# Decoding the first batch's weights through a PSUM bank, with attention in one bank

## The chip, the cores and the metric

One core of one Trainium2 chip. The metric is the device time of one execution in microseconds; a few runs are made and their median counts. Five engines work side by side, each through its own list of instructions in a fixed order: TensorE (matmuls), VectorE, ScalarE, GpSimd, and SyncE, which issues the DMAs. Where one needs what another makes, it waits for that engine's count of finished instructions (a semaphore). PSUM has eight banks of 128 partitions x 512 words of 32 bits; TensorE writes its results there, VectorE and ScalarE can read and write them.

## What is computed

Windowed attention (4 batches, 8 heads, 576 positions, 64 per head; four heads see a window of 32, four a dilated one of 128 by steps of 4), then a gated feed-forward block, then a second one with a PReLU:

```
attn = softmax(mask(q @ k.T / 8));  x = attn @ v            # reshaped to 2304 x 512
y    = (sigmoid(x @ w_gate) * (x @ w_val)) @ w_out           # 512 -> 1536 -> 512
h    = y @ w_in;  g = max(h, 0) + alpha * min(h, 0)          # 512 -> 2048
out  = g @ w_out2                                            # 2048 -> 512
```

The weights come as raw words, two of 32 bits for each number (the 64-bit form of it). The kernel turns them into 32-bit floats itself.

## The kernel before

**Decoding.** `decode` (L175) takes one or more blocks of 128 x 512 numbers, as pairs of a destination `d` in SBUF and the words `w`, whose low and high halves lie in turn. Three VectorE steps make a number: L179 shifts the high word left by 3 and masks it into `d`; L183 adds the two top bits of the high word to `d`; L187 adds the three top bits of the low word, shifted down. Each step is done for all blocks of the call before the next begins. The first batch decodes 36 such blocks: `dec` for the 12 column groups of the gate and value weights (two blocks each; the first group as two calls), `odec` for `w_out` (three blocks for each of four groups; the second as two calls and one). So there are 18 calls. Later batches decode `w_in` and `w_out2` with the same function.

**What follows on a decoded block.** ScalarE squares and sums it (`wb`, L194), TensorE adds that over the partitions with a matmul against ones (`wsum`, L148), VectorE makes a power of two from the sum (`wpow`, L156 and L160, then GpSimd L164), and ScalarE and GpSimd, or ScalarE and VectorE, split the scaled weights into two halves of 16 bits (`spl`, L168, L172, L204, L205). `g` and `v` are TensorE's matmuls of gate and value (L590, in two halves of 12 matmuls), `sig` and `mul` ScalarE's sigmoid and VectorE's product (L603, L608), `half` the split of the product, `o` the output matmuls (L632).

**Attention.** A head group `hb` is one of two kinds of one batch; 0 and 1 belong to the first batch, 2 and 3 to the second, and these are done while the first batch goes through its feed-forward block. `qkm hb c` puts a third of the scores into a bank (L309, L316, L323), `qks hb c` takes their maximum and subtracts it on VectorE (L354, L355), `pvm hb half` multiplies by the values for two pairs of heads (L437), and `pvx hb half pair` splits the result on ScalarE and VectorE (L171, L172).

**Banks.** Banks 0 to 5 are three double buffers for the feed-forward matmuls; the small sums of L148 sit at the end of one of them. Banks 6 and 7 are attention's, in turn (`att_bank`).

**Order.** In the first batch the order of all engines' work is written out by hand in `FIRST`, a list of tasks; each engine gets its instructions in that order. From the second batch on loops set it, and the preparation of the later weights is dealt out by a budget.

Of the kernel before, what the change touches and what calls it, by code (L numbers as in the profile page):

```python
# [1563 lines left out]
warm 8 5; lqk 0 3; lqk 1 3; lv 0; qkm 0 0; lv 1; qks 0 0; qkm 0 1; qkm 0 2; exp 0 0; qks 0 1 1; rs 0 0;  # L1564
qks 0 2 1; exp 0 1; pm 0 0 0; qkm 1 0 4; tr 0 0; rs 0 1; lgv 0; qks 1 0; pm 0 1 0; exp 0 2; rs 0 2; qkm 1 1 5;
exp 1 0; lgv 1; lqk 2; warm 6 2; lv 3; pm 0 2 0; qkm 1 2 0; lal; qks 1 1; tr 0 2; exp 1 1; xb 0; tr 0 1;
qks 1 2 1; rs 1 1; pv32 0 0 6; pm 1 1 0; xb 1; rs 1 0; xsum 0 0; exp 1 2; pm 1 0 0; pv32 0 1 4; dec 0 0; xpow 0;
rs 1 2; pm 1 2 0; tr 1 1; vhi 1 1; dec 0 1; tr 1 0; lgv 2; phi 1 1; vlo 1 1; vhi 1 0; pvx 0 1 1; warm 14 3;
tr 1 2; pvx 0 1 0; pvx 0 0 1; lv 2; wb 0; vlo 1 0; wsum 0; pvx 0 0 0; phi 1 0; plo 1 1; phi 1 2; plo 1 2 0;
plo 1 0 0; wpow 0; spl 0 0; pvm 1 1 4; pvm 1 0; dec 1; pvx 1 1 1; pvx 1 0 0; lgv 3; spl 0 1 1; pvx 1 1 0;  # L1570
g 0 0 0; wb 1; wsum 1; lgv 4; lgv 6; wgs 0; wpow 1; pvx 1 0 1; qkm 2 0; qkm 2 1; dec 2; xb 2; lgv 5; spl 1 0;
spl 1 1 1; g 0 0 1; wb 2; v 0 0 0; sig 0 0; wsum 2 0; v 0 0 1; wgs 1; wpow 2; dec 3; mul 0 0; g 0 1 0; g 0 1 1;
spl 2 0; spl 2 1 1; wb 3; wsum 3; v 0 1 0; xb 3; wpow 3; v 0 1 1; spl 3 0; sig 0 1; g 0 2 0; qks 2 1; g 0 2 1;
# [104 lines left out]
```

## Time and profile before

| | |
|---|---|
| median of 3 runs | 900.86 us (900.86 to 901.72) |
| profiled execution | 900.97 us |
| its span (first to last instruction) | 899.2 us |
| TensorE busy | 850.2 us (95%) |
| VectorE busy | 681.9 us (76%) |
| ScalarE busy | 450.4 us (50%) |
| GpSimd busy | 304.6 us (34%) |

All rows below are of the one profiled execution; times count from the start of its span, and 1.8 us of the execution lie outside the span. Busy time is an average over the whole span, and the stretches differ much, so the rows are of stretches. Durations of instructions that follow each other on one engine overlap a little in the records where neither waits for the other.

### The profile page before, as it was taken

The numbers are of one execution on the slowest core, as the hardware profiler recorded it, in microseconds if no ns is written. First come the engines' busy times: TensorE is split into PE (matmuls) and PEld (weight loads), VectorE is DVE, ScalarE is ACT, GpSimd is POOL, SyncE is SP. The second block draws the span as 40 slices with busy tenths as digits, with TensorE's granted clock in tenths as the row PEclk, the third lists the DMA queues.
The fourth block names the chain that finished last, engine by engine and source line by source line (L and its number), as shares of the span: only waits on it lengthen the run. The fifth ranks groups of instructions, "written<-read, shape, count | busy, mean of one in ns | idle before, by whom it ended". The sixth has DMA issues, their size and how long they took to land.

```text
span 899.2 us, 19438 instructions
## 1 busy us (share of the span) xinstructions
PE 850.2 (95%) x8196; PEld 701.5 (78%) x8196; DVE 681.9 (76%) x1039; ACT 450.4 (50%) x739; POOL 304.6 (34%) x264
## 2 busy tenths in 40 slices
PE   7879789799999999999999989997899999999998
...
GB/s 323 266 212 151 121 141 158 58 28 141 139 51 182 144 74 195 62 1 230 266 180 219 300 279 195 347 218 184 265 236 188 240 322 188 199 274 203 142 214 83
DMA packets 85176, 166.81 MB, mean 186 GB/s; under 512 B 5345, under 2 KB 57697, under 8 KB 85089
## 3 DMA queue, kind: packets, MB, share of 16 engines
...
q14 instruction: 24, 0.19, 0.1%
...
## 4 chain that ended last, share of the span: by engine, by line
PE 57%; DVE 26%; ACT 6%; issue 4%; DMA 4%; POOL 1%; SPq 1%; ACTq 0%; DVEq 0%; POOLq 0%
PE banks L590 14%; PE banks L1207 14%; PE banks L964 13%; PE banks L632 12%; DVE plain L183 4%; DVE plain L187 3%; PE banks L437 3%; DVE plain L179 2%; DVE temp_w L1010 2%; DVE temp_y L1010 1%; DVE gf L608 1%; DVE halves L824 1%; DMA words<-w_gate 1%; DVE g_gv L1049 1%; PE banks L323 1%
## 5 line engine op out<-in xcount | busy, mean ns | idle before, releaser
L590 PE MATMUL banks<-xh,w_gv 128*128 128x288 f16 x2304 | 297.7, 291 | 1.5 <-ACT sg L603 1.5
L590 PEld LDWEIGHTS <-w_gv 128*128 128x128 f16 x2304 | 226.1, 99 | 62.6 <-issue 1.8
L964 PE MATMUL banks<-yh,w_i 128*128 128x256 f16 x1536 | 189.9, 275 | 12.1 <-ACT temp_y L1019 6.4
L964 PEld LDWEIGHTS <-w_i 128*128 128x128 f16 x1536 | 151.3, 99 | 32.5 <-issue 12.3
L632 PE MATMUL banks<-gt,w_o 128*128 128x288 f16 x1152 | 149.5, 291 | 1.0 <-POOL gt L168 0.9
L632 PEld LDWEIGHTS <-w_o 128*128 128x128 f16 x1152 | 113.5, 100 | 31.9 <-issue 1.1
L1207 PEld LDWEIGHTS <-g_gv 128*128 128x128 f16 x780 | 76.7, 98 | 9.1
L1207 PE MATMUL banks<-w,g_gv 128*128 128x256 f16 x612 | 75.5, 273 | 0.0
L164 POOL TENSOR_SCALAR sc<-sc 128x1 f32<-128x1 f32 x35 | 12.4, 354 | 180.7 <-DVE sc L160 180.6
L1059 POOL TENSOR_TENSOR yh<-temp_y 128x512 f32<-128x512 f32 x16 | 27.0, 1689 | 131.6 <-DVE temp_y L1010 126.9
L194 ACT ACTIVATE junk<-plain 128x1024 bf16<-128x1024 f32 (+1 forms) x36 | 36.4, 1010 | 60.4 <-DVE plain L198 32.1
L1010 DVE SCALAR_TENSOR_TENSOR temp_w<-neg,sc,temp_w 128x256 f32<-128x256 f32 x48 | 55.5, 1195 | 10.9 <-ACT neg L1002 10.8
L187 DVE SCALAR_TENSOR_TENSOR plain<-words,plain 128x512 uint32<-128x512 uint32 x68 | 61.9, 931 | 1.2
L183 DVE SCALAR_TENSOR_TENSOR plain<-words,plain 128x512 uint32<-128x512 uint32 x68 | 59.3, 893 | 1.2
L1207 PEld LDWEIGHTS <-g_g 128*128 128x128 f16 x564 | 55.2, 98 | 6.4
L168 POOL TENSOR_TENSOR gt<-gf,gt 128x576 f16<-128x576 f32 x24 | 36.8, 1533 | 65.2 <-ACT gt L615 65.2
L608 DVE SCALAR_TENSOR_TENSOR gf<-banks,sg 128x576 f32<-128x576 f32 x48 | 36.0, 750 | 29.3 <-PE banks L590 28.9
L603 ACT ACTIVATE sg<-banks,sc 128x576 f32<-128x576 f32 x48 | 35.2, 734 | 35.1 <-PE banks L590 24.7
L615 ACT ACTIVATE gt<-gf 128x576 f16<-128x576 f32 x48 | 32.3, 675 | 38.3 <-DVE gf L608 38.3
L1207 PE MATMUL banks<-w,g_g 128*128 128x256 f16 x396 | 48.3, 273 | 0.0
L179 DVE TENSOR_SCALAR plain<-words 128x512 uint32<-128x512 uint32 x68 | 40.2, 612 | 8.9 <-DMA plain_dram<-plain 5.5
L388 POOL TENSOR_TENSOR s<-s,rs 128x1152 f32<-128x1152 f32 (+1 forms) x9 | 17.8, 1975 | 71.7 <-DVE rs L383 64.4
...
## 6 DMA issues: line engine op xcount, KB each, us to landing
...
```

The source lines that it names most:

```text
L168: engine.tensor_tensor(out=lo, in0=src, in1=hi, op=ALU.subtract)
L179: nc.vector.tensor_scalar(out=d, in0=hi, scalar1=3, scalar2=0x3FFFFFFF, op0=ALU.logical_shift_left, op1=ALU.bitwise_and)
L183: nc.vector.scalar_tensor_tensor(out=d, in0=hi, scalar=0xC0000000, in1=d, op0=ALU.bitwise_and, op1=ALU.bitwise_or)
L187: nc.vector.scalar_tensor_tensor(out=d, in0=lo, scalar=29, in1=d, op0=ALU.logical_shift_right, op1=ALU.bitwise_or)
L194: nc.scalar.activation(junk[:, :src.shape[1]], src, AF.Square, accum_out=dst)
L590: nc.tensor.matmul(ps[:, h, :], lhsT=a, rhs=x_[:, H2 * h:H2 * h + H2], start=(kk == 0 and i == 0), stop=(kk == KD - 1 and i == 2),)
L603: nc.scalar.activation(halves(sg), ps, AF.Sigmoid, scale=sgx[b][:, m:m + 1])
L608: nc.vector.scalar_tensor_tensor(out=halves(gf), in0=ps, scalar=2.0 ** -15, in1=halves(sg), op0=ALU.mult, op1=ALU.mult)
L632: nc.tensor.matmul(ps[:, h, :], lhsT=a, rhs=x_[:, H2 * h:H2 * h + H2], start=(m == 0 and z == 0), stop=(m == M1 - 1 and z == 2),)
L964: nc.tensor.matmul(o, lhsT=h, rhs=l, start=(new and v == 0 and q == 1), stop=(q == total_), skip_group_check=True,)
L1010: nc.vector.scalar_tensor_tensor(out=temps[x_][:, c], in0=t[:, c], scalar=slope[:, u + v:u + v + 1], in1=src[:, c], op0=ALU.mult, op1=ALU.add,
L1207: nc.tensor.matmul(ps[:, H4 * t:H4 * t + H4].rearrange("p (c f) -> p c f", c=2), lhsT=a, rhs=x_, start=(first and k == 0 and t == 0 and z ...
```

## The change

In the first batch (`turn["first"]`) `decode` works on one block after the other. It cuts each block into two halves of 256 columns, and the words wait in a PSUM bank between the steps: the first step writes the bank, the second reads and writes it, the third reads it and writes the destination in SBUF. The two halves alternate step by step. The bank is number 2 for the first calls and number 6 from the task `one` on, which stands before the scores of head group 2; from there to the task `one 0`, near the end of `FIRST`, attention has bank 7 alone. Later batches decode as before.

```diff
@@ -91,7 +91,7 @@
 
 
     banks = psum.tile([P, 8, 512], F32, name="banks")
-    turn = {"m": -1, "a": -1, "h": -1, "first": True}
+    turn = {"m": -1, "a": -1, "h": -1, "first": True, "words": 2, "one": False}
 
     holds = {}
     begun = set()
@@ -120,7 +120,7 @@
 
     def att_bank(key, spare=None):
         if spare is None:
-            turn["a"] = (turn["a"] + 1) % 2
+            turn["a"] = 1 if turn["one"] else (turn["a"] + 1) % 2
             spare = 6 + turn["a"]
         hold(spare, key)
         waiting.add(key)
@@ -175,6 +175,26 @@
     def decode(*pairs):
 
         pairs = [(d.bitcast(U32), w[:, :, :, 0], w[:, :, :, 1]) for d, w in pairs]
+        if turn["first"]:
+
+            hold(turn["words"], "words")
+            t = banks[:, turn["words"], :].bitcast(U32).rearrange("p (k f) -> p k f", k=4)
+            for pair in pairs:
+                parts = [(t[:, k:k + 2],) + tuple(x_[:, k:k + 2] for x_ in pair) for k in (0, 2)]
+                for t_, d, lo, hi in parts:
+                    nc.vector.tensor_scalar(
+                        out=t_, in0=hi, scalar1=3, scalar2=0x3FFFFFFF, op0=ALU.logical_shift_left,
+                        op1=ALU.bitwise_and,
+                    )
+                for t_, d, lo, hi in parts:
+                    nc.vector.scalar_tensor_tensor(
+                        out=t_, in0=hi, scalar=0xC0000000, in1=t_, op0=ALU.bitwise_and, op1=ALU.bitwise_or
+                    )
+                for t_, d, lo, hi in parts:
+                    nc.vector.scalar_tensor_tensor(
+                        out=d, in0=lo, scalar=29, in1=t_, op0=ALU.logical_shift_right, op1=ALU.bitwise_or
+                    )
+            return
         for d, lo, hi in pairs:
             nc.vector.tensor_scalar(
                 out=d, in0=hi, scalar1=3, scalar2=0x3FFFFFFF, op0=ALU.logical_shift_left, op1=ALU.bitwise_and
@@ -420,16 +440,16 @@
         pv_mm(hb, half)
         pv_x(hb, half)
 
-    def pv_mm(hb, half, spare=None):
+    def pv_mm(hb, half, spare=None, only=None):
         b, kind = divmod(hb, 2)
         v_ = vh[hb]
         first, last = (0, NB // 2) if half == 0 else (NB // 2, NB)
         ops = [(m, max(m, first), min(m + 2, last)) for m in range(max(first - 1, 0), last)]
-        tiles = []
-        for pair in range(2):
+        tiles = xt.setdefault((hb, half), [None, None])
+        for pair in range(2) if only is None else (only,):
             k = slice(64 * pair, 64 * pair + 64)
             ps = att_bank(("pv", hb, half, pair), None if spare is None else spare + pair)[:, :H2]
-            tiles.append(ps)
+            tiles[pair] = ps
             for z, (m, n0, n1) in enumerate(ops):
                 p_ = [p_half(hb, i, WINDOW * (m + n0 + 1), WINDOW * (m + n1 + 1))[k] for i in range(2)]
                 w = [v_[k, i, m].rearrange("p h d -> p (h d)") for i in range(2)]
@@ -438,7 +458,6 @@
                         ps[:, WINDOW * (n0 - first):WINDOW * (n1 - first)], lhsT=a, rhs=x_,
                         start=(z == 0 and i == 0), stop=(z == len(ops) - 1 and i == 2), skip_group_check=True,
                     )
-        xt[hb, half] = tiles
 
     def pv32_mm(hb, half, spare):
 
@@ -1242,6 +1261,11 @@
 
     engines = (nc.gpsimd, nc.vector)
 
+    def one_bank(on=1):
+
+        turn["one"] = bool(on)
+        turn["words"] = 6
+
     def part(i):
         return whole if i is None else thirds[i]
 
@@ -1267,6 +1291,8 @@
         "vhi": v_hi,
         "vlo": v_lo,
         "pvm": pv_mm,
+        "pvo": lambda hb, half, only: pv_mm(hb, half, None, only),
+        "one": one_bank,
         "pv32": pv32_mm,
         "pvx": pv_x,
```

`FIRST` is written with other line breaks, so a comparison of its lines says little. The tasks of attention that moved, in their order (everything between them keeps its order):

```
before: ... qkm 2 0; qkm 2 1 ... qks 2 1 ... qks 2 0 ... qkm 2 2 ... qks 2 2
after:  ... one; qkm 2 0 ... qks 2 0 ... qkm 2 1 ... qks 2 1 ... qkm 2 2 ... qks 2 2

before: ... pvm 2 0 ... pvx 2 0 0 ... pvx 2 0 1; pvm 2 1 ... pvx 2 1 0; g 0 9 0; wpow 11; qkm 3 0 ... pvx 2 1 1
after:  ... pvo 2 0 0 ... pvx 2 0 0; pvo 2 0 1 ... pvx 2 0 1; pvo 2 1 0 ... pvx 2 1 0; pvo 2 1 1 ... pvx 2 1 1; qkm 3 0

before: ... qks 3 0 ... qkm 3 1 ... qkm 3 2; odec 1 2; qks 3 1; wgs 11; qks 3 2; v 0 10 0
after:  ... qks 3 0; qkm 3 1 ... odec 1 2; qks 3 1; qkm 3 2; wgs 11; v 0 10 0; qks 3 2
```

VectorE, the decoding of column group 3 of gate and value, before. In brackets stand the engines or DMA queues whose count a row waits for; x2 means two equal rows, and the engine's own name (DVE) a wait for an earlier instruction of VectorE itself.

```order
L160 TENSOR_SCALAR sc<-sc 128x1 [waits DVE_49]
L179 TENSOR_SCALAR plain<-words 128x512 [waits DMAHW2_49,Pool_49]
L179 TENSOR_SCALAR plain<-words 128x512 [waits DMAHW3_49]
L183 SCALAR_TENSOR_TENSOR plain<-words,plain 128x512 [waits DVE_49] x2
L187 SCALAR_TENSOR_TENSOR plain<-words,plain 128x512 [waits DVE_49] x2
L608 SCALAR_TENSOR_TENSOR gf<-banks,sg 128x576 [waits PE_49,Activation_49]
```

The same place after. `banks` is PSUM.

```order
L160 TENSOR_SCALAR sc<-sc 128x1 [waits DVE_49]
L185 TENSOR_SCALAR banks<-words 128x256 [waits DMAHW2_49]
L185 TENSOR_SCALAR banks<-words 128x256 [waits DVE_49]
L190 SCALAR_TENSOR_TENSOR banks<-words,banks 128x256 [waits DVE_49] x2
L194 SCALAR_TENSOR_TENSOR plain<-words,banks 128x256 [waits DVE_49,Pool_49]
L194 SCALAR_TENSOR_TENSOR plain<-words,banks 128x256
L185 TENSOR_SCALAR banks<-words 128x256 [waits DMAHW3_49,DVE_49]
L185 TENSOR_SCALAR banks<-words 128x256 [waits DVE_49]
L190 SCALAR_TENSOR_TENSOR banks<-words,banks 128x256 [waits DVE_49] x2
L194 SCALAR_TENSOR_TENSOR plain<-words,banks 128x256 [waits DVE_49]
L194 SCALAR_TENSOR_TENSOR plain<-words,banks 128x256
L627 SCALAR_TENSOR_TENSOR gf<-banks,sg 128x576 [waits PE_49,Activation_49]
```

Six instructions have become twelve of half the size. The sixth and the twelfth wait for nothing, the first for its load; the others wait for VectorE itself. In the built program each of these waits counts up to the instruction right ahead, where before a second or third step waits for the one two places ahead.

TensorE, the first scores of head group 3 (L316, L323) and what stands behind them, before: matmuls of the gate (L590).

```order
L316 LDWEIGHTS mask_sb
L316 MATMUL banks<-mask_sb 128x64
L323 MATMUL banks<-k,q 64x64 [waits DMAHW5_49,DMAHW4_49]
L323 MATMUL banks<-k,q 64x64 x11
L590 LDWEIGHTS w_gv_1237
L590 MATMUL banks<-xh,w_gv_1237 128x288
```

After, where these lines have the numbers L336, L343 and L609:

```order
L336 LDWEIGHTS mask_sb
L336 MATMUL banks<-mask_sb 128x64
L343 MATMUL banks<-k,q 64x64 [waits DMAHW5_49,DMAHW4_49]
L343 MATMUL banks<-k,q 64x64 x11
L329 LDWEIGHTS mask_sb
L329 MATMUL banks<-mask_sb 128x384 [waits DVE_49]
L336 LDWEIGHTS mask_sb
L336 MATMUL banks<-mask_sb 128x64
L343 MATMUL banks<-k,q 64x64 x12
L609 LDWEIGHTS w_gv_1291
```

The second third of the scores, with its wait for VectorE, now stands right behind the first, ahead of the gate's matmuls.

## Rows read from the trace of the kernel before

**Rows 1.** Sums of windows; columns: stretch, length, busy us (instructions) by engine, clock, DMA.
```profile
20.00:176.00 156.00, 130.15 (x1251) 98.02 (x1248) 149.05 (x222) 97.97 (x159) 89.33 (x79) 0.85 0.49 165
180.00:200.00 20.00, 20.00 (x227) 16.15 (x226) 3.87 (x6) 7.04 (x12) 0.92 (x4) 0.99 0.09 31
```

**Rows 2.** Chain of waits within 19.7 to 176 us, shares by line.
```profile
by line: DVE plain L183 19.4%; DVE plain L187 14.5%; DVE plain L179 11.0%; issue 7.3%; DMA words<-w_gate 6.2%; PE banks L590 6.0%; PE banks L437 5.4%; DVE gf L608 3.9%; DMA words<-w_val 2.9%; DVE w_o L172 2.7%; DVE plain L198 2.6%; DVE vh L
```

**Rows 3.** Groups by line, VectorE, 19.7 to 176 us; xcount | busy us, mean ns | idle.
```profile
L183 DVE SCALAR_TENSOR_TENSOR plain<-words,plain 128x512 uint32<-128x512 uint32 x36 | 36.1, 1043 | 0.1
L187 DVE SCALAR_TENSOR_TENSOR plain<-words,plain 128x512 uint32<-128x512 uint32 x36 | 34.8, 1006 | 0.1
L179 DVE TENSOR_SCALAR plain<-words 128x512 uint32<-128x512 uint32 x36 | 21.9, 647 | 0.9 <-DMA words<-w_gate 0.6 <-DMA words<-w_val 0.3
```

**Rows 4.** Timeline, VectorE: start us, us, line; a call of two blocks.
```profile
69.51 0.75 DVE L179 TENSOR_SCALAR plain<-words 128x512 uint32<-128x512 uint32 x2
70.17 1.29 DVE L183 SCALAR_TENSOR_TENSOR plain<-words,plain 128x512 uint32<-128x512 uint32 x2
71.38 1.29 DVE L187 SCALAR_TENSOR_TENSOR plain<-words,plain 128x512 uint32<-128x512 uint32 x2
```

**Rows 5.** Timeline, all engines, from 53 us.
```profile
53.42 2.25 DVE L183 SCALAR_TENSOR_TENSOR plain<-words,plain 128x512 uint32<-128x512 uint32 x2
...
53.66 1.47 POOL L168 TENSOR_TENSOR w_gv<-plain,w_gv 128x512 f16<-128x512 f32 x1 [1.58 <-ACT w_gv L205]
```

**Rows 6.** Forms by line over the whole run: duration ns min/median/max, starts, forms.
```profile
L179 DVE TENSOR_SCALAR plain<-words x68: 412/423/2347, 19.7 to 474.5; 128x512 uint32<-128x512 uint32 x68
...
L183 DVE SCALAR_TENSOR_TENSOR plain<-words,plain x68: 672/693/1776, 20.4 to 475.0; 128x512 uint32<-128x512 uint32 x68
...
L608 DVE SCALAR_TENSOR_TENSOR gf<-banks,sg x48: 695/751/760, 49.8 to 510.4; 128x576 f32<-128x576 f32 x48
...
L354 DVE TENSOR_REDUCE mx<-s x12: 552/553/553, 200.9 to 400.0; 128x6 f32<-128x384 f32 x12
L354 DVE TENSOR_REDUCE mx<-banks x9: 517/548/557, 6.9 to 139.8; 128x6 f32<-128x384 f32 x9
```

**Rows 7.** Timeline, VectorE, 136 to 149 us: a lone block, head group 3, the product.
```profile
136.79 0.61 DVE L179 TENSOR_SCALAR plain<-words 128x512 uint32<-128x512 uint32 x1
137.43 0.69 DVE L183 SCALAR_TENSOR_TENSOR plain<-words,plain 128x512 uint32<-128x512 uint32 x1
138.16 0.69 DVE L187 SCALAR_TENSOR_TENSOR plain<-words,plain 128x512 uint32<-128x512 uint32 x1
...
139.83 0.55 DVE L354 TENSOR_REDUCE mx<-banks 128x6 f32<-128x384 f32 x1
...
148.11 0.69 DVE L608 SCALAR_TENSOR_TENSOR gf<-banks,sg 128x576 f32<-128x576 f32 x1
```

**Rows 8.** Timeline, TensorE and then VectorE, 105 to 115 us.
```profile
105.77 2.77 PE L437 MATMUL banks<-s,vh 64*128 64x64 f16 x54
108.46 6.41 PE L590 MATMUL banks<-xh,w_gv 128*128 128x288 f16 x36
...
112.89 0.81 DVE L172 SCALAR_TENSOR_TENSOR xh<-banks,xh 128x288 f16<-128x288 f32 x2
114.96 0.16 DVE L156 TENSOR_SCALAR sc<-banks 128x1 uint32<-128x1 uint32 x1 [1.26 <-PE banks L148]
```

**Rows 9.** Timeline, TensorE, 130 to 148 us.
```profile
130.76 0.48 PE L309 MATMUL banks<-mask_sb 128*128 128x384 bf16 x1 [3.83 <-DVE xh L172]
...
132.71 3.06 PE L590 MATMUL banks<-xh,w_gv 128*128 128x288 f16 x12
...
135.69 0.48 PE L309 MATMUL banks<-mask_sb 128*128 128x384 bf16 x1
...
137.05 10.46 PE L590 MATMUL banks<-xh,w_gv 128*128 128x288 f16 x84
147.35 0.19 PE L148 MATMUL banks<-sc,mask_sb 128*128 128x1 bf16 x2
```

More of the change, by code (lines that the diff above doesn't have):

```diff
@@ L1563 @@
 FIRST = """
[L1564 to L1573, printed above, removed]
@@ new lines @@
+1 0; xb 1; rs 1 0; xsum 0 0; exp 1 2; pm 1 0 0; pv32 0 1 4; dec 0 0; xpow 0; rs 1 2; pm 1 2 0; tr 1 1; vhi 1 1; dec 0
+1; tr 1 0; lgv 2; phi 1 1; vlo 1 1; vhi 1 0; pvx 0 1 1; warm 14 3; tr 1 2; pvx 0 1 0; pvx 0 0 1; lv 2; wb 0; vlo 1 0;
+wsum 0; pvx 0 0 0; phi 1 0; plo 1 1; phi 1 2; plo 1 2 0; plo 1 0 0; wpow 0; spl 0 0; pvm 1 1 4; pvm 1 0; dec 1; pvx 1
+1 1; pvx 1 0 0; lgv 3; spl 0 1 1; pvx 1 1 0; g 0 0 0; wb 1; wsum 1; lgv 4; lgv 6; wgs 0; wpow 1; pvx 1 0 1; one; qkm 2
+0; dec 2; xb 2; lgv 5; spl 1 0; spl 1 1 1; g 0 0 1; wb 2; v 0 0 0; sig 0 0; wsum 2 0; v 0 0 1; wgs 1; wpow 2; dec 3;
@@ new lines @@
+mul 0 0; g 0 1 0; g 0 1 1; spl 2 0; spl 2 1 1; wb 3; wsum 3; v 0 1 0; xb 3; wpow 3; v 0 1 1; spl 3 0; sig 0 1; g 0 2
+0; qks 2 0; g 0 2 1; qkm 2 1; spl 3 1; dec 4; wb 4; mul 0 1; wgs 2; wsum 4; v 0 2 0; qks 2 1; sig 0 2; qkm 2 2; lgv
+10; half 0 0 1; wpow 4; half 0 1 1; spl 4 0; dec 5; g 0 3 0; v 0 2 1; wb 5; lqk 3; wsum 5 0; qks 2 2; spl 4 1 1; lgv
+7; xsum 1; g 0 3 1; wgs 3; wpow 5; mul 0 2; dec 6; v 0 3 0; wgs 4; lo 0 0; g 0 4 0; exp 2; sig 0 3; spl 5 0 1; v 0 3
+1; wb 6; xpow 1; spl 5 1 1; wsum 6; half 0 2 1; g 0 4 1; v 0 4 0; wpow 6; v 0 4 1; mul 0 3; lgv 8; g 0 5 0; lo 1 0;
@@ new lines @@
+half 0 3; spl 6 0; sig 0 4; wgs 5; dec 7; mul 0 4; spl 6 1; wb 7; g 0 5 1; rs 2; wsum 7; wgs 6; vhi 2 1; pm 2; wpow 7;
+sig 0 5; spl 7 0; spl 7 1; dec 8; v 0 5 0; tr 2; v 0 5 1; mul 0 5; g 0 6 0; wb 8; g 0 6 1; lgv 9; phi 2; lv 4; wsum 8;
+v 0 6 0; wpow 8; plo 2; half 0 4; sig 0 6; v 0 6 1; g 0 7 0; vlo 2 1; g 0 7 1; spl 8 0; dec 9; half 0 5 1; vhi 2 0;
+vlo 2 0; mul 0 6; spl 8 1 1; wgs 7; v 0 7 0; wgs 8; wb 9; lo 0 2; half 0 6 1; wsum 9 0; sig 0 7; pvo 2 0 0; wpow 9; v
+0 7 1; spl 9 0; g 0 8 0; dec 10; spl 9 1 1; mul 0 7; pvx 2 0 0; pvo 2 0 1; lgv 11; lo 1 1; g 0 8 1; wb 10; wsum 10; v
@@ new lines @@
+0 8 0; pvx 2 0 1; pvo 2 1 0; v 0 8 1; wpow 10; sig 0 8; dec 11; spl 10 0 1; mul 0 8; spl 10 1; wgs 9; wgs 10; wb 11;
+wsum 11; lo 0 1; pvx 2 1 0; pvo 2 1 1; g 0 9 0; wpow 11; half 0 7 1; spl 11 0; odec 0 0 1 2; orow 0 1 1; g 0 9 1; v 0
+9 0; spl 11 1; lo 1 2; pvx 2 1 1; qkm 3 0; orow 0 0 0; lo 2 1; lo 2 2; qks 3 0; qkm 3 1; orow 0 2 0; odec 1 0 1; obd 0
+0; obd 0 1; sig 0 9; g 0 10 0; half 0 8 1; orow 1 1 0; v 0 9 1; osum 0; opow 0; mul 0 9; odec 1 2; qks 3 1; qkm 3 2;
+wgs 11; v 0 10 0; qks 3 2; vhi 3 0; vhi 3 1; g 0 10 1; v 0 10 1; orow 1 0 0; g 0 11 0; orow 1 2 0; lo 2 0; lqk 4; ospl
@@ new lines @@
+0 0; half 0 9 1; vlo 3 1; g 0 11 1; sig 0 10; obd 1 0; mul 0 10; v 0 11 0; vlo 3 0; v 0 11 1; exp 3; obd 1 1; sig 0
+11; osum 1; rs 3; mul 0 11; opow 1; half 0 11 1; lo 3 1; ospl 0 1; odec 2 0 1 2; o 0 0 0; half 0 10 1; lo 3 0; lo 3 2;
+orow 2 1 1; orow 2 0 1; ospl 1 0 1; orow 2 2 0; obd 2 0; pm 3; o 0 0 1; tr 3; o 0 0 2; obd 2 1; o 0 0 3; gs 1; ospl 1
+1; oy 0 0; osum 2; opow 2; odec 3 0 1 2; phi 3; ospl 2 0 1; orow 3 1 1; plo 3 0 0; ospl 2 1; o 0 1 0; orow 3 2 0; lv
+5; orow 3 0 0; obd 3 1; o 0 1 1; o 0 1 2; obd 3 0; o 0 1 3; alpha; one 0; pvm 3 0; o 0 2 0; o 0 2 1; pvx 3 0 1; pvx 3
@@ L1596 @@
+0 0; osum 3; opow 3; oy 0 1; pvm 3 1; o 0 2 2; pvx 3 1 1; ospl 3 0 1; ospl 3 1 1; o 0 2 3; o 0 3 0; o 0 3 1; xb 4; o 0
+3 2; oy 0 2; v 1 0 0; g 1 0 0; pvx 3 1 0; qkm 4 0; o 0 3 3; oy 0 3; g 1 0 1; v 1 0 1; sig 1 0; qks 4 0; mul 1 0
 """
```

25 lines of the change are left out of this document (3 added, 22 removed).

## The prediction, made before the changed kernel ran

> **What bounds the kernel now.** I read the sums of windows first. [...] So the first stretch is VectorE's and what follows is TensorE's. The chain of waits for the first stretch says the same: its three largest shares are the three lines of `decode` [rows 2]. A microsecond more or less on VectorE before 176 us moves the start of the TensorE part, and with it the end, by about a microsecond.
>
> The groups by line give the decoding in that stretch: 36 blocks of 128x512 words, three instructions each, busy 21.9, 36.1 and 34.8 us, together 92.8 us [rows 3]. Instructions that don't wait for each other overlap by some 0.07 us in these records (two of 0.68 us take 1.29 us, and the next line starts 1.21 us after them [rows 4]); counted from start to start, with 54 such overlaps left (18 calls by three lines), that is 92.8 - 54 x 0.07 = 89.0 us, or 2.47 us for a block.
>
> Undisturbed a block takes far less: two blocks in 69.51 to 72.67 us, 3.16 us, are 1.58 us each [rows 4]. The rest is stalls: two instructions that take 1.29 us there take 2.25 us while GpSimd runs a 128x512 subtraction [rows 5]. By the mean durations (647, 1043, 1006 ns against 420, 680, 680 undisturbed) the stalls are 36 x (0.227 + 0.363 + 0.326) = 33.0 us. Who is hit can be read from the forms: L183, with both inputs in SBUF, has a median of 693 ns and a longest of 1776; L608, with one input in PSUM, ran 48 times, 12 of them in this stretch, between 695 and 760 ns [rows 6]. So an instruction with an input in PSUM isn't stalled by GpSimd, and the changed decoding should lose nearly all 33 us of stalls. The question is what it pays.
>
> **Part 1, the decoding.** A block becomes six instructions of 128x256. None of these forms is in the trace, so I size them by neighbours. One column costs (751 - 548) / 192 = 1.06 ns between L354 at 384 columns and L608 at 576 (medians), and 256 columns come to 548 - 128 x 1.06 = 0.413 us; the same line gives 0.683 us at 512, which is L183 undisturbed, so it holds for SBUF and PSUM inputs alike [rows 6].
>
> What counts is the distance from start to start. In the order before, the second and third steps of two blocks alternate and each waits for the instruction two places ahead: distance 0.605 us at a duration of 0.68, 0.075 less [rows 4]. Where a block is decoded alone each step waits for the one just ahead: 136.79 + 0.61 to 137.43, and 137.43 + 0.69 to 138.16, so 0.035 us more than the duration [rows 7]. The changed code alternates two halves, but both halves lie in one bank, and in the built program every instruction of a block except the sixth, and the first of a call, waits for VectorE's own count up to the instruction right ahead of it, even the second shift, which reads nothing that the first one writes. So four distances within a block are 0.413 + 0.035 = 0.448 us, one is 0.413 - 0.075 = 0.338 us, and the last is 0.448 where another block follows in the same call (18 times) and 0.338 where none does (18 times). Sum: 162 x 0.448 + 54 x 0.338 = 72.6 + 18.3 = 90.8 us, against 89.0 us. The decoding comes out 1.8 us dearer: the halving gives back all that the stalls cost.
>
> Bounds. The shift writes SBUF now and takes 0.42 us for 512 columns [rows 6], less than a column per 1.06 ns; at that pace 256 columns would be 0.42 - 256 x 0.53 ns = 0.28 us, and 72 shifts save 72 x 0.13 = 9.4 us more. I take the slow value, because every row with PSUM in it runs at 1.06 ns a column, L354 too, which like the shift has one input. Upwards: no row has VectorE write PSUM. One form, L608, spreads from 695 to 751 ns; that much again, 0.06 us, on the four instructions of a block that write or on the four that read PSUM is 144 x 0.06 = 8.6 us.
>
> [...]
>
> GpSimd, which is stopped by VectorE just as well, gets through its subtractions sooner (1.47 us where both wait [rows 5]); fewer of them then meet VectorE's other two-input instructions. I put that at -1 us, with one stall in [rows 5] being about that, and keep -4 and +2 as its ends.
>
> **Part 2, attention in one bank.** Only `qk` and `pv` of heads 2 and 3 change. For the scores of head 2 I count nothing: in `FIRST` a call of two blocks (4.9 us at 2.47 each) lies on VectorE between one third and the next, and TensorE needs 1.4 to 2 us to fill the bank (b, below). Three places do cost.
>
> (a) `pv` of head 2. Before, both pairs are multiplied in one go (54 matmuls, 2.77 us, so 1.4 us a pair), then come 36 matmuls of gate and value in 6.41 us, 2.1 us per 12 [rows 8]. Now the second pair waits until VectorE has read the first, which by the old order is done at about 113.3 us, the middle of the two in 112.89 to 113.70. Then come 1.4 us for the pair and 2.1 us for 12 matmuls queued behind it, and only then the sum of L148 for which VectorE's next step waits: 116.8 us, where that step now starts at 114.96 [rows 8]. At the pace of the 84 matmuls in [rows 9], 0.125 us each instead of 0.178, it is 1.0 + 1.5 us and 115.8. So between 0.8 and 2.0 us; I take 1.3.
>
> (b) First scores of head 3. Before, they lie ready in the other bank. Now TensorE may start them only after VectorE has read the last `pv`, and VectorE's next instruction waits for them: 1.36 us (135.69 to 137.05) where TensorE came from work, 1.95 us (130.76 to 132.71) where it came from an idle stretch of 3.83 us [rows 9]. I take 1.7.
>
> (c) Third scores of head 3. VectorE ends the second at 139.83 us [rows 7]; before, TensorE had the third ready since 137.05 and ran ahead with 84 matmuls of gate and value until 147.35 [rows 9], for which the multiply at 148.11 waits [rows 7]. Now the third starts at about 139.9, and the 84 matmuls stand behind it on TensorE: 139.9 + 1.36 + 10.3 + 0.1 = 151.7 us. That is 3.6 us later, less only if VectorE itself is late, and more if a slower pace follows TensorE's new idle stretch: 36 of the 84 at 0.178 us would add 1.9, so 5.5 is the upper end.
>
> These are covered by nothing: TensorE's 25.9 us of idle time lie elsewhere, and at each place VectorE has no other work ahead of the wait. Queues besides: the loads on SyncE keep their order; a block's first half of buffers is freed some 2.5 us earlier than now, which only helps.
>
> **Sum.** 900.97 us of the profiled execution (span 899.2 and 1.8 outside it; the median of the runs is 900.86, so 0.1 less) + 1.8 - 1.0 + 1.3 + 1.7 + 3.6 = 908.4 us; I say 908.
>
> **The rivals.**
> 1. The single bank costs nothing, since TensorE has 25.9 us to spare [rows 1] and the order was rewritten around it: 900.97 + 1.8 - 1.0 = 901.8 us. For it: most waits of TensorE end well before VectorE needs the result. Against it: (c), where TensorE has 0.7 us in hand before the multiply, not 4.
> 2. The other side, faster: the halves overlap in spite of the waits. Place: the 162 distances inside the blocks. Price: at 0.338 us each 162 x 0.11 = 17.8 us less, 908.4 - 17.8 = 890.6 us. It decides from the point where a distance is under some 0.39 us, 9 us less in all. For it: the 0.605 us of [rows 4]. Against it: the waits, and 0.035 us over the duration where a wait stands [rows 7].
> 3. The shift keeps its fast rate into PSUM: 908.4 - 9.4 = 899.0 us. For it the 0.42 us in [rows 6], against it the pace of all rows with PSUM.
> 4. PSUM is dearer for VectorE than SBUF: 908.4 + 8.6 = 917 us. Against it L354, which takes 548 ns from PSUM and 553 ns from SBUF [rows 6]; for it that no row writes PSUM. [...]
> 5. The change doesn't take the stalls away, because the words themselves are still read from SBUF: 908.4 + 33, some 940 us. L608's narrow spread [rows 6] speaks against it.
>
> **How the numbers follow.** Forecast (903 to 914) 0.50, rival 1 0.13, rival 2 0.10, rival 3 0.10, rival 4 0.12, rival 5 0.03, the rest 0.02. The range from 897 to 917 leaves out rival 2, rival 5 and half of rival 4. A measurement of this kernel tells about 0.2% from no change, here 899.1 to 902.7 us. Below that: rival 2, 0.06 of rival 3, 0.03 of rival 1 and the rest, 0.21. Within: 0.04 of rival 3 and 0.10 of rival 1, 0.14. Above: the forecast, rivals 4 and 5, 0.65.
>
> **What would show it.** The three lines of the decoding with durations near 0.41 us, no long ones among them, and distances near 0.45 us; their share of the chain hardly changed; TensorE waiting for VectorE in the scores of head 3, and VectorE for TensorE at the maximum and the multiply behind them; VectorE's stretch ending some 7 us after 176 us, and the same shift at the end. Distances well under 0.4 us, shifts of 0.28 us, or no new waits of VectorE at (a) to (c) would prove me wrong, and so would a TensorE part after 176 us that isn't simply shifted.

## The result, and the profile after

The changed kernel took 914.13 us (median of 4 runs, 913.12 to 915.45), the kernel before 901.29 us beside it (4 runs, 900.86 to 901.96): ratio 1.0143, interval 1.0124 to 1.0161, slower by 12.8 us. The profiled execution took 913.2 us with a span of 911.4 us, 12.2 us more than the span before. Line numbers below are those of the changed kernel: `decode`'s three steps in the new branch L185, L190, L194 (before L179, L183, L187), product L627 (L608), maximum and difference of the scores L374 and L375 (L354, L355), gate and value matmuls L609 (L590), scores L329 to L343, `pv` L457, outputs L651 (L632).

The sums of windows, after, answer to [rows 1]:

```profile
20.00:187.00 167.00, 132.00 (x1241) 98.84 (x1239) 145.11 (x329) 97.77 (x156) 72.53 (x79) 0.85 0.46 154
190.00:210.00 20.00, 20.00 (x215) 16.04 (x215) 4.48 (x7) 7.03 (x12) 0.92 (x4) 0.98 0.09 31
```

The stretch is 11 us longer, TensorE stands idle for 35 us of it instead of 25.9, and VectorE for 21.9 us instead of 7. What follows is TensorE's as before. VectorE was the bound before; now it waits too.

Groups by line, VectorE, 19 to 187 us, answering to [rows 3]:

```profile
L190 DVE SCALAR_TENSOR_TENSOR banks<-words,banks 128x256 uint32<-128x256 uint32 x72 | 30.9, 429 | 2.5
L185 DVE TENSOR_SCALAR banks<-words 128x256 uint32<-128x256 uint32 x72 | 30.7, 426 | 2.1 <-DMA words<-w_gate 0.3
L194 DVE SCALAR_TENSOR_TENSOR plain<-words,banks 128x256 uint32<-128x256 uint32 x72 | 27.1, 418 | 2.0
```

The spread of one of these lines over its starts (min/median/max ns), answering to [rows 6]:

```profile
L190 DVE SCALAR_TENSOR_TENSOR banks<-words,banks x72: 428/428/448, 20.1 to 180.8; 128x256 uint32<-128x256 uint32 x72
```

The stalls are gone: none of the 72 starts of L190 took over 448 ns, where L183 reached 1776. So is the pace that stood against them: a call of two blocks, timeline of VectorE, answering to [rows 4]:

```profile
47.78 0.88 DVE L185 TENSOR_SCALAR banks<-words 128x256 uint32<-128x256 uint32 x2
48.69 0.89 DVE L190 SCALAR_TENSOR_TENSOR banks<-words,banks 128x256 uint32<-128x256 uint32 x2
49.69 0.75 DVE L194 SCALAR_TENSOR_TENSOR plain<-words,banks 128x256 uint32<-128x256 uint32 x2
50.47 0.89 DVE L185 TENSOR_SCALAR banks<-words 128x256 uint32<-128x256 uint32 x2
51.40 0.89 DVE L190 SCALAR_TENSOR_TENSOR banks<-words,banks 128x256 uint32<-128x256 uint32 x2
52.33 0.75 DVE L194 SCALAR_TENSOR_TENSOR plain<-words,banks 128x256 uint32<-128x256 uint32 x2
```

Each pair of halves takes 0.88 or 0.89 us, two full durations and a little, because the second half waits for the first. Only the third step's pair overlaps (0.75). A block is 2.6 us.

The three places in attention, timelines of VectorE, answering to [rows 7] and [rows 8]; the brackets are idle time and what ended it:

```profile
112.81 0.45 DVE L172 SCALAR_TENSOR_TENSOR xh<-banks,xh 128x288 f16<-128x288 f32 x1
114.71 0.46 DVE L172 SCALAR_TENSOR_TENSOR xh<-banks,xh 128x288 f16<-128x288 f32 x1 [1.46 <-ACT xh L171]
115.89 0.16 DVE L156 TENSOR_SCALAR sc<-banks 128x1 uint32<-128x1 uint32 x1 [0.72 <-PE banks L148]
...
132.05 0.45 DVE L172 SCALAR_TENSOR_TENSOR xh<-banks,xh 128x288 f16<-128x288 f32 x1
133.86 0.56 DVE L374 TENSOR_REDUCE mx<-banks 128x6 f32<-128x384 f32 x1 [1.36 <-PE banks L343]
...
144.16 0.56 DVE L375 TENSOR_TENSOR s<-banks,mx 128x384 f32<-128x384 f32 x1
146.88 0.56 DVE L374 TENSOR_REDUCE mx<-banks 128x6 f32<-128x384 f32 x1 [2.16 <-PE banks L343]
...
152.92 0.76 DVE L627 SCALAR_TENSOR_TENSOR gf<-banks,sg 128x576 f32<-128x576 f32 x1 [3.57 <-PE banks L609]
...
158.80 0.76 DVE L627 SCALAR_TENSOR_TENSOR gf<-banks,sg 128x576 f32<-128x576 f32 x1 [1.30 <-PE banks L148]
```

The rows up to 115.89 belong to (a), those of 132.05 and 133.86 to (b), those from 144.16 on to (c). The starts of `dec 10` and of the first scores' maximum, before, and of `dec 10` after, for the counting further down:

```profile
106.40 1.88 DVE L179 TENSOR_SCALAR plain<-words 128x512 uint32<-128x512 uint32 x2
...
130.63 0.54 DVE L354 TENSOR_REDUCE mx<-banks 128x6 f32<-128x384 f32 x1
```
```profile
106.26 0.88 DVE L185 TENSOR_SCALAR banks<-words 128x256 uint32<-128x256 uint32 x2
```

TensorE's timeline at (c), answering to [rows 9]:

```profile
144.77 0.48 PE L329 MATMUL banks<-mask_sb 128*128 128x384 bf16 x1 [5.41 <-DVE s L375]
...
145.28 1.55 PE L343 MATMUL banks<-k,q 128*64 128x64 f32 x24
146.76 11.90 PE L609 MATMUL banks<-xh,w_gv 128*128 128x288 f16 x84
158.50 0.19 PE L148 MATMUL banks<-sc,mask_sb 128*128 128x1 bf16 x2
```

At 144.77 TensorE has been idle for 5.41 us until VectorE had read the second scores; then the third scores and the 84 matmuls follow, and the product at 158.80 waits for the end of these. The granted clock there, in two windows (the column ahead of the last two, as a share of full speed; in windows of 0.4 us it is 0.50 up to 149.6 us and 1.00 from 150.0 us on):

```profile
144.80:152.00 7.20, 7.20 (x58) 5.29 (x58) 2.44 (x3) 0.65 (x2) 3.29 (x2) 0.66 0.58 199
152.00:158.50 6.50, 6.50 (x56) 5.19 (x54) 3.88 (x5) 6.21 (x9) 0.00 (x0) 1.00 0.38 140
```

The 84 matmuls before, where TensorE came from work:

```profile
137.10:147.30 10.20, 10.20 (x86) 8.15 (x85) 10.06 (x11) 8.79 (x12) 7.94 (x7) 1.00 0.83 279
```

TensorE's matmuls, numbered in order, lie 10.7 us later than before from 182 us until batch 3 ends at about 530 us. Then the distance grows to 12.2 us, in the stretch where the outputs of the last batch give way to the next layer. That stretch, before and then after:

```profile
526.00:549.00 23.00, 19.73 (x158) 15.87 (x156) 13.94 (x23) 15.10 (x30) 11.06 (x14) 0.93 0.67 226
```
```profile
536.70:561.00 24.30, 20.95 (x155) 16.22 (x153) 13.46 (x23) 15.06 (x30) 11.00 (x14) 0.86 0.66 220
```

The mean granted clock is 0.93 before and 0.86 after. In windows of 1 us it lies at 0.50 to 0.54 from 532 to 535 us before and at 0.50 from 542.7 to 548.7 us after; but for the windows at the edges of these (0.75; 0.78 and 0.80) the rest is at 1.00. These are one execution each; the last section says why this can't be put down to the change.

### The profile page after: what moved, and what is told of

Same layout as the page of the kernel before. It is cut to its first block, busy times and chain, and to the rows that moved or that the text cites. A ratio compares the mean times of both kernels' runs of the same rounds, so it can differ in the third digit from the quotient of the medians.

```text
span 911.4 us, 19569 instructions
## 1 busy us (share of the span) xinstructions
PE 854.6 (94%) x8196; PEld 703.7 (77%) x8196; DVE 676.7 (74%) x1147; ACT 450.7 (49%) x739; POOL 287.7 (32%) x264
## 4 chain that ended last, share of the span: by engine, by line
PE 57%; DVE 27%; ACT 6%; DMA 4%; issue 4%; SPq 1%; POOL 1%; DVEq 0%; ACTq 0%; POOLq 0%
PE banks L609 15%; PE banks L1226 14%; PE banks L983 13%; PE banks L651 12%; DVE banks L190 3%; DVE banks L185 3%; DVE plain L194 2%; DVE temp_w L1029 2%; PE banks L457 2%; DMA words<-w_gate 2%; DVE halves L843 2%; DVE temp_y L1029 1%; DVE gf L627 1%; PE banks L343 1%; DMA w_dram<-halves 1%
## 5 line engine op out<-in xcount | busy, mean ns | idle before, releaser
L609 PE MATMUL banks<-xh,w_gv 128*128 128x288 f16 x2304 | 299.4, 292 | 1.5 <-ACT sg L622 1.5
L609 PEld LDWEIGHTS <-w_gv 128*128 128x128 f16 x2304 | 227.0, 100 | 63.6 <-issue 1.8
L651 PE MATMUL banks<-gt,w_o 128*128 128x288 f16 x1152 | 149.3, 291 | 1.0 <-POOL gt L168 0.9
L651 PEld LDWEIGHTS <-w_o 128*128 128x128 f16 x1152 | 113.4, 99 | 31.9 <-issue 1.1
L164 POOL TENSOR_SCALAR sc<-sc 128x1 f32<-128x1 f32 x35 | 10.0, 286 | 199.2 <-DVE sc L160 199.2
L627 DVE SCALAR_TENSOR_TENSOR gf<-banks,sg 128x576 f32<-128x576 f32 x48 | 36.1, 752 | 33.7 <-PE banks L609 31.9
L168 POOL TENSOR_TENSOR gt<-gf,gt 128x576 f16<-128x576 f32 x24 | 33.5, 1396 | 66.7 <-ACT gt L634 66.7
L1082 POOL TENSOR_TENSOR temp_w<-temp_w,yh 128x512 f32<-128x512 f32 (+1 forms) x20 | 29.8, 1489 | 34.6 <-DVE g_g L1068 19.7
L1068 DVE SCALAR_TENSOR_TENSOR g_gv<-temp_w,sc,g_gv 128x256 f16<-128x256 f32 (+1 forms) x37 | 25.6, 701 | 18.2 <-ACT g_gv L1064 18.0
L1021 ACT ACTIVATE neg<-temp_w 128x512 f32<-128x512 f32 x24 | 15.1, 630 | 42.2 <-DVE temp_w L1041 32.3
```

Of the source, the lines that this page charges most:

```text
L168: engine.tensor_tensor(out=lo, in0=src, in1=hi, op=ALU.subtract)
L609: nc.tensor.matmul(ps[:, h, :], lhsT=a, rhs=x_[:, H2 * h:H2 * h + H2], start=(kk == 0 and i == 0), stop=(kk == KD - 1 and i == 2),)
L627: nc.vector.scalar_tensor_tensor(out=halves(gf), in0=ps, scalar=2.0 ** -15, in1=halves(sg), op0=ALU.mult, op1=ALU.mult)
L651: nc.tensor.matmul(ps[:, h, :], lhsT=a, rhs=x_[:, H2 * h:H2 * h + H2], start=(m == 0 and z == 0), stop=(m == M1 - 1 and z == 2),)
L1082: add(out=a12, in0=a12, in1=s2, op=ALU.subtract)
```

## The experiments

Medians in us. The kernel before ran again beside each group of runs, with medians of 901.66 (e1, e2, e4, e5), 901.18 (e3, e7, e8), 901.40 (e6, e9, e10) and 900.14 (e11, e12). Across groups the distances to these are compared, not the bare medians.

| run | decoding | order | us | ratio to before |
|---|---|---|---|---|
| changed kernel | halves in PSUM | changed | 914.1 | 1.0143 [1.0124, 1.0161] |
| e1_one_bank | SBUF, as before | changed | 912.1 | 1.0123 [1.0096, 1.0151] |
| e2_whole | whole blocks in PSUM | changed | 900.4 | 0.9989 [0.9973, 1.0005] |
| e4_two_banks | halves, 4 of 36 blocks in two banks | changed | 911.1 | 1.0104 [1.0087, 1.0121] |
| e5_shift_sbuf | shift in SBUF, then PSUM | changed | 907.9 | 1.0068 [1.0053, 1.0084] |
| e3_third | halves | (c) moved | 910.5 | 1.0100 [1.0083, 1.0117] |
| e6_whole_c | whole | (c) moved | 896.1 | 0.9930 [0.9907, 0.9954] |
| e7_whole_bc | whole | (b) and (c) | 897.8 | 0.9959 [0.9945, 0.9972] |
| e8_whole_abc | whole | (a), (b), (c) | 900.4 | 0.9993 [0.9983, 1.0003] |
| e9_whole_b2c | whole | (b) otherwise, (c) | 893.0 | 0.9897 [0.9872, 0.9922] |
| e10_whole_a2b2c | whole | all three, otherwise | 891.7 | 0.9882 [0.9852, 0.9911] |
| e11_halves_a2b2c | halves | as e10 | 904.4 | 1.0046 [1.0031, 1.0061] |
| e12_sbuf_a2b2c | SBUF, as before | as e10 | 905.3 | 1.0058 [1.0038, 1.0078] |

**e1_one_bank**, the single bank by itself:

```
-        if turn["first"]:
+        if False:
```

> The changed order and attention's single bank stay, the words of the weights stay in SBUF and are decoded as in the kernel before (three instructions of 128x512 a block, two blocks interleaved). Theory (both parts of the change cost, the single bank more): VectorE waits of about 1 us at the pv of head 2, 1.4 at the first scores of head 3, and the product mul 0 11 5 to 6 us later after the third scores, so about 909 us (906 to 912), with VectorE's stalls back (means of the three decoding lines near 1.0, 1.0 and 0.65 us). Rival (the single bank costs nothing, the whole loss lies in the decoding): 901 to 902 us.

912.1 us: the rival falls, and the size is 3 us over the theory. The single bank comes with the changed order here; no run has one without the other. TensorE's gate and value matmuls, numbered in order, are where they were until 87 us (-0.1 us), then 3.7 us late at 123 and 11.6 at 182. The waits are those of the changed kernel and one more; VectorE at `opow 0`, and the 24 matmuls of TensorE that it waited for:

```profile
141.29 0.16 DVE L156 TENSOR_SCALAR sc<-banks 128x1 uint32<-128x1 uint32 x1 [3.06 <-PE banks L148]
```
```profile
136.06 5.14 PE L609 MATMUL banks<-xh,w_gv 128*128 128x288 f16 x24
```

Their granted clock is 0.58; the same 24 took 3.11 us at 1.00 in the changed kernel. So in these two executions the parts don't add: the bank alone moves the matmuls by 11.6 us at 182 us, bank and halves together by 10.7. The wait at `opow 0` may be the execution's and not the variant's, as e6_whole_c shows below.

**e2_whole**, a block in one piece:

```
-                parts = [(t[:, k:k + 2],) + tuple(x_[:, k:k + 2] for x_ in pair) for k in (0, 2)]
+                parts = [(t,) + tuple(pair)]
```

> The changed kernel, but each block's words go through the PSUM bank in one piece: three instructions of 128x512 instead of six of 128x256, one block after the other. Theory (each instruction costs a fixed part and 0.035 us of waiting for the one ahead, 1.06 ns a column beyond it): durations 0.70 us, distances 0.735 us, 2.2 us a block instead of 2.6, so 36 x 0.4 = 14 us less than the changed kernel, about 900 us (897 to 903). Rival (PSUM makes VectorE slower by the column or by the instruction's read and write): durations of 0.8 us and more, 2.5 us a block, 911 to 914 us. Rival (GpSimd stalls the longer instructions again, as it does in SBUF): durations up to 1.7 us, above 914 us.

900.4 us, as the theory had it, and not to be told from the kernel before (0.9973 to 1.0005). The three lines over their starts, and one block in the timeline:

```profile
L185 DVE TENSOR_SCALAR banks<-words x36: 667/694/704, 19.5 to 164.8; 128x512 uint32<-128x512 uint32 x36
```
```profile
L190 DVE SCALAR_TENSOR_TENSOR banks<-words,banks x36: 695/696/710, 20.3 to 165.6; 128x512 uint32<-128x512 uint32 x36
```
```profile
L194 DVE SCALAR_TENSOR_TENSOR plain<-words,banks x36: 686/686/692, 21.0 to 166.3; 128x512 uint32<-128x512 uint32 x36
```
```profile
47.78 0.69 DVE L185 TENSOR_SCALAR banks<-words 128x512 uint32<-128x512 uint32 x1
48.51 0.70 DVE L190 SCALAR_TENSOR_TENSOR banks<-words,banks 128x512 uint32<-128x512 uint32 x1
49.24 0.69 DVE L194 SCALAR_TENSOR_TENSOR plain<-words,banks 128x512 uint32<-128x512 uint32 x1
```

Distances 0.73 us at a duration of 0.70, so 2.2 us a block; no stalls. Halving columns took a duration from 0.696 to 0.428 us, so half the columns cost 0.61 of the time, and each start adds its wait of 0.035 us. Much of what this gains is lost again where attention has one bank: `dec 10` starts at 98.31 us, 8.1 us earlier than in the kernel before, but at 182 us TensorE's matmuls are only 3.0 us earlier.

**e4_two_banks**, for the four blocks of the first calls (banks 2 and 3):

```
+            t2 = banks[:, 3 if turn["words"] == 2 else 6, :] ...
+                    (t_[:, k:k + 2],) + tuple(x_[:, k:k + 2] for x_ in pair) for t_, k in ((t, 0), (t2, 2))
```

> The changed kernel, but in the early calls (decoding of column blocks 0 and 1, four blocks of words) the two halves lie in two PSUM banks; the later 32 blocks are as in the changed kernel. Theory (the halves wait for each other only because they share a bank): distances within these four blocks fall from 0.463 to 0.338 us, 2.03 us a block instead of 2.6, in all some 2 us, about 912 us. Rival (the distance of 0.46 us is what VectorE needs for these forms whatever waits stand in front): distances stay at 0.46 us and the time at 914 us.

911.1 us, about what the theory said, and the two blocks of `dec 1`, timeline of VectorE:

```profile
30.63 0.74 DVE L188 TENSOR_SCALAR banks<-words 128x256 uint32<-128x256 uint32 x2
31.29 0.75 DVE L193 SCALAR_TENSOR_TENSOR banks<-words,banks 128x256 uint32<-128x256 uint32 x2
31.95 0.74 DVE L197 SCALAR_TENSOR_TENSOR plain<-words,banks 128x256 uint32<-128x256 uint32 x2
32.61 0.74 DVE L188 TENSOR_SCALAR banks<-words 128x256 uint32<-128x256 uint32 x2
33.26 0.74 DVE L193 SCALAR_TENSOR_TENSOR banks<-words,banks 128x256 uint32<-128x256 uint32 x2
33.92 0.74 DVE L197 SCALAR_TENSOR_TENSOR plain<-words,banks 128x256 uint32<-128x256 uint32 x2
```

A pair every 0.66 us: 1.97 us a block instead of 2.6. In the built program the halves in one bank wait for the instruction right ahead, in two banks for the one two places ahead. So the distance of 0.46 us comes with the shared bank and the wait that stands in the program for it; VectorE can do the forms faster. Whether two halves in one bank would overlap without that wait, no run tried.

**e5_shift_sbuf**: as e2_whole, with the shift's result in `d`, read there by the second step.

> As the variant with whole blocks of 128x512, but the shift writes its result to SBUF (as in the kernel before), the second step reads only SBUF and writes the PSUM bank, the third reads the bank. This shows which operand in PSUM keeps GpSimd's stalls away. Theory A (any operand in PSUM is enough): the second step has 0.70 us throughout, the shift is fast (0.42 us) where GpSimd rests and stalled elsewhere (mean 0.65): 0.69 + 2 x 0.735 = 2.15 us a block, 1 to 3 us under the variant with whole blocks, about 898 us. Theory B (only an input in PSUM helps): the second step has a mean near 1.0 us with a longest over 1.5 us, 36 x 0.3 = 11 us over that, about 909 us.

907.9 us, near theory B. The second step, both inputs in SBUF and the output in PSUM:

```profile
L190 DVE SCALAR_TENSOR_TENSOR banks<-words,plain x36: 699/701/2747, 20.5 to 174.7; 128x512 uint32<-128x512 uint32 x36
```

Its group by line has a mean of 992 ns. For this step, which has two inputs, the output in PSUM didn't keep the stalls away; one input in PSUM did (e2_whole, longest 710 ns, and 692 for L194 with its output in SBUF). For the shift, which has one input, the output was enough: with its input in SBUF and its output in PSUM it took at most 704 ns in e2_whole, with both in SBUF up to 2347 here, at a shortest of 410.

**e3_third**, the repair of (c):

```
- qks 3 1; qkm 3 2; wgs 11; v 0 10 0; qks 3 2; vhi 3 0; vhi 3 1; g 0 10 1; v 0 10 1
+ qks 3 1; wgs 11; v 0 10 0; g 0 10 1; qkm 3 2; v 0 10 1; qks 3 2; vhi 3 0; vhi 3 1
```

> The changed kernel with one thing moved in the order: the matmuls of the third scores of head 3 stand behind half of v 0 10 and all but the end of g 0 10 (two times 12 matmuls) instead of ahead of them. Theory (term c: the 84 matmuls stood behind these scores, and after TensorE's wait of 5 us they ran at the lower clock): TensorE works through its wait, most of the 84 matmuls are done earlier, the product mul 0 11 comes 3 to 5 us sooner, about 910 us (908 to 912). Rival (VectorE itself is late by then, so that another of its waits takes the place): 913 to 914 us.

910.5 us, as the theory had it: 3.7 us less. TensorE after the second scores:

```profile
139.66 3.10 PE L609 MATMUL banks<-xh,w_gv 128*128 128x288 f16 x24
145.20 0.32 PE L329 MATMUL banks<-mask_sb 128*128 128x384 bf16 x1 [2.44 <-DVE s L375]
...
146.36 7.52 PE L609 MATMUL banks<-xh,w_gv 128*128 128x288 f16 x60
```

24 of the 84 matmuls run ahead of the third scores, TensorE's wait is 2.44 instead of 5.41 us, and the other 60 go at a granted clock of 1.00 (7.52 us, 0.125 each; the 84 took 11.90, 0.142 each). The product `mul 0 11` comes at 154.02 instead of 158.80.

**e7_whole_bc**, whole blocks, (c) as in e3_third, and `odec 1 0 1` ahead of `qks 3 0; qkm 3 1`:

> Whole blocks in the PSUM bank, and two repairs of the order: the third scores of head 3 as in the run that moves them alone, and the decoding of two blocks of the output weights ahead of the reduction of the first scores of head 3, so that VectorE has work while TensorE fills the bank. Theory (terms b and c are waits that order alone makes): 1.4 + 3 to 5 us less than whole blocks alone, which ran 900.4: about 895 us (893 to 897). Rival (the single bank itself is too narrow): 899 us or more.

897.8 us: neither figure. The wait of 1.36 us at the first scores went, and a larger one came at `opow 0`:

```profile
134.44 0.16 DVE L156 TENSOR_SCALAR sc<-banks 128x1 uint32<-128x1 uint32 x1 [6.90 <-PE banks L148]
```

The second scores' matmuls were now late, and on TensorE they stand ahead of 24 matmuls and the sum that `opow 0` reads; these 24 took 4.81 us, where they took 3.12 in e2_whole.

**e8_whole_abc** adds, at (a): `dec 10` split, the read of the first pair of `pv` between its halves, the second pair's matmuls ahead of `g 0 8 0`, the sum of block 10 behind the next `pv`.

> As the run before, and a third repair: the two blocks of decoding dec 10 apart, with VectorE's read of the first pair of pv of head 2 between them, so that TensorE can compute the second pair meanwhile. Theory (term a: VectorE waits 1.5 us for xh and 1.6 us for the sum of L148 there in the variant with whole blocks): 2 to 3 us less than with the other two repairs, about 892.5 us (890 to 895). Rival (ScalarE's part of that read comes late where its queue is full): no gain, 895 us.

900.4 us, a miss; the theory's price was for the waits removed, and VectorE got another in their place:

```profile
110.35 0.16 DVE L156 TENSOR_SCALAR sc<-banks 128x1 uint32<-128x1 uint32 x1 [3.72 <-PE banks L148]
```

The sum that `wpow 10` reads now stood behind two `pv` on TensorE.

**e6_whole_c**, (c) alone on whole blocks:

> Whole blocks in the PSUM bank with only the third scores of head 3 moved (term c), the first scores as in the changed kernel. In the run with both moved, VectorE waited 6.9 us for the sum of osum 0, since the decoding ahead of the first scores made the second scores and the 24 matmuls behind them late on TensorE. Theory (that wait is the second move's own, term c is worth its 3.4 us here too): no wait over 1.5 us at osum 0, and 900.4 - 3.4 = 897.0 us or a little less (895.5 to 898). Rival (VectorE's progress is bounded by TensorE anyway at that point): 899 to 901 us.

896.1 us, in the theory's range. The trace has a wait of 2.72 us at `opow 0`, which the theory did not have. Up to there the order is that of e2_whole, whose trace has no such wait; what differs is the pace of the 24 matmuls ahead of the sum, 4.93 us here and 3.12 there. Windows of the two, this run first:

```profile
128.20:133.00 4.80, 4.80 (x29) 3.20 (x29) 2.14 (x4) 0.41 (x1) 1.04 (x1) 0.62 0.30 83
```
```profile
125.90:129.00 3.10, 3.10 (x29) 2.49 (x28) 2.89 (x5) 1.27 (x2) 0.34 (x1) 1.00 0.00 0
```

The granted clock is 0.62 in one and 1.00 in the other. So one execution can have a wait of 2 to 3 us that another with the same work up to that point doesn't have; the profiled execution here was also the slowest of the five, 899.1 us.

**e9_whole_b2c**: as e7_whole_bc, but `qkm 3 1` behind `osum 0`.

> Whole blocks, the third scores moved, and the decoding of two blocks ahead of the first scores' reduction, now with the second scores' matmuls behind osum 0 on TensorE, so that they hold nothing up. Theory (term b is a wait of 1.4 us that other work can fill, and the wait of 6.9 us came from TensorE's order alone): no wait at the first scores nor at osum 0, 1.4 us less than with the third scores alone, 894 to 896.5 us. Rival (ScalarE's bound of the output weights, which osum 0 sums, is what is late): a wait of VectorE of several us at osum 0 remains, 897 us or more.

893.0 us: 3.1 less than e6_whole_c, more than the 1.4 us. In the profiled executions the wait at `opow 0` shrank to 0.76 us as well; whether that makes the difference of the medians isn't shown.

**e10_whole_a2b2c** adds, at (a), `wb 10; wsum 10` ahead of `pvo 2 0 1`, and `wpow 10; dec 11 0` ahead of `pvx 2 0 1`.

> As the variant with both scores moved, and at pv of head 2 VectorE takes the scale of column block 10 and the first half of the decoding of block 11 before it reads the second pair. Theory (term a: 1.5 and 1.6 us of waiting there are a matter of order): both waits go, some 3 us less, 891 to 893.5 us. Rival (the words of block 11 have not landed by then, or what follows on TensorE comes later): 894 us or more.

891.7 us, inside the theory's range, but against e9_whole_b2c the median gains 1.4 us of the 3 expected, and the runs of the two overlap (890.4 to 893.7 and 891.2 to 893.4), so the gain isn't clear of noise. The waits of 2.04 and 2.14 us at (a) went, and two others came: 0.81 us for ScalarE's part of `spl 10` and 1.77 us at the product behind it, for TensorE. In the traces TensorE is 1.9 us earlier at 182 us; the later stretch where the clock differs, below, took that back in the profiled execution. This is the best version, 9.7 us under the kernel before.

**e11_halves_a2b2c** and **e12_sbuf_a2b2c** put that order to the other two decodings.

> The changed kernel's decoding (halves of 128x256 in one bank) in the order with all three repairs. Theory (decoding and order are separate costs: the order is worth the 8.7 us between whole blocks with and without repairs, the halves 2.6 - 2.2 us a block): 914.1 - 8.7 = 905.4 us (904 to 908), still slower than the kernel before. Rival (VectorE, later by the halves, leaves TensorE more time, so the repairs are worth less here): 909 to 911 us.

> The decoding in SBUF as in the kernel before, attention in one bank, the order with all three repairs. Theory (the single bank costs by its order alone): 912.1 - 8.7 = 903.4 us, within some 3 us of the kernel before (901 to 905). Rival (one bank costs in itself): 907 us or more. Against the variant with whole blocks in PSUM and this order (891.7) it shows what GpSimd's stalls are worth: theory 36 x (2.47 - 2.2) = 10 us.

904.4 us, as the theory had it, and 905.3 us, 1.9 over the theory's figure and just outside its range. In the repaired order halves in PSUM and words in SBUF come out alike, 4.3 and 5.2 us over the kernel before, and whole blocks, 9.7 us under it, are 14 to 15 us better than both. The theory put the stalls at 10 us there. With the words in SBUF one bank and the best order found still cost 5 us (0.38 to 0.78%), where e1_one_bank costs 10.4: the order explains about half of that; what makes the rest isn't settled.

## Why the prediction was right, and where its sizes were off

The direction and the mechanism held: the stalls went, the halving gave back what they had cost, and one bank of attention cost the rest. 914.1 us lies 6 us above the 908 predicted, inside the range of 897 to 917 and at the very end of the forecast's own 903 to 914. The loss is 13 us where 7.4 was forecast, so the range did some of the work. By its terms:

- **Decoding, +1.8 us.** It was +4.3. The waits are where the built program showed them: 0.463 us from start to start behind a wait, 0.338 us without, and 162 x 0.463 + 54 x 0.338 = 93.3 us where the prediction had 90.8, against 89.0. The wait itself is the 0.035 us of [rows 7]; the duration was mis-sized, 0.428 us instead of the 0.413 taken by the column from [rows 6].
- **Rival 2** (the halves overlap) fell: 0.463 us in the changed kernel. e4_two_banks shows it true of halves in two banks; in one bank, with the waits that stand there, it is false.
- **Rival 3** (the shift's fast rate) fell: L185 has a mean of 426 ns for 256 columns, 690 for 512 in e2_whole, where L179 took 423 undisturbed with the target in SBUF. No run shows the 0.53 ns a column in this rival's price, since none has the shift on 256 columns with its target in SBUF; into PSUM it took (690 - 426) / 256 = 1.03 ns a column.
- **Rival 4** (PSUM dearer) fell as a price of 0.06 us on each access: 0.428 is 0.015 over the estimate, and L190 with PSUM on both sides takes 0.696 us in e2_whole, where L183 took 0.69 undisturbed. L194, which reads PSUM and writes SBUF, takes 0.686 us there.
- **Rival 5** (the stalls stay) fell by the 448 ns.
- **Relief, -1.0 us.** VectorE's other two-input instructions lost 2.6 us: nine of L172 to `w_gv` take 6.7 us instead of 7.8, four of L302 to `vh` 6.3 instead of 7.8. Only the first fits the reason given, that GpSimd is done sooner: its subtractions for `w_gv` (L168, 15 of 128x512) took 1594 ns in the median before and 1162 after. In e1_one_bank, with the words back in SBUF, `w_gv` takes 7.8 us again, but `vh` 5.6, so its gain isn't the decoding's; it may be the order's. The stretch also began 0.5 us earlier, with a load.
- **(a), +1.3 us.** From the start of `dec 10` to `wpow 10` it is 9.6 us (106.26 to 115.89), before 8.6 (106.40 to 114.96): +1.0.
- **(b), +1.7 us.** Idle for 1.36 us at 133.86: +1.4.
- **(c), +3.6 us, at most 5.5.** From the end of the second scores' last step to the product it is 14.1 us (144.16 + 0.56 to 158.80), before 8.2 (139.91 to 148.11): +5.9. The end of the range came true, and for its reason: after TensorE's 5.41 us of idle time the scores took 1.99 us instead of 1.36, and the 84 matmuls 11.90 instead of 10.46. From 144.80 to 152.00 us, which holds these scores and the first of the 84, the granted clock was 0.66; for the 84 before (137.1 to 147.3 us) it was 1.00. e3_third takes 3.7 us of it back by order alone. This and the decoding are the mis-sized terms.
- **Rival 1** (one bank costs nothing) fell by e1_one_bank, 912.1 us. It gets nearer in the repaired order, 905.3 us or 5.2 over the kernel before.
- **That the end is simply shifted** was wrong by 1.5 us in the profiled executions: the stretch near 530 us. Whether the change made that isn't shown (last section).
- **The whole.** The terms, 4.3 - 2.6 - 0.5 + 1.0 + 1.4 + 5.9 = 9.5, lie 1.2 us under the 10.7 us seen at 182 us. Counted along VectorE nothing is left over, and it shows when the loss arises. `dec 10` starts 0.1 us earlier than before, so the first 20 of the 36 blocks cost nothing on balance. Then come 1.1 us at (a); 0.9 us over the five blocks of `dec 11` and `odec 0` and what lies between them; 1.4 us at (b); 1.6 us over the three blocks of `odec 1`; and 5.9 us at (c). That is 10.7 us at the product (158.80 against 148.11), and the last six decoded blocks add nothing more. The single bank's three places make 8.4 us of it, where the prediction had 6.6.

What the decoding in halves costs against words in SBUF isn't settled by the whole runs: it is 2 us more in the changed order and 1 us less in the repaired one, and in both the intervals overlap. That the changed kernel lacks the wait of e1_one_bank at `opow 0` would fit that TensorE catches up while VectorE is late, but such a wait also came and went between e2_whole and e6_whole_c with the clock alone.
